# Retention and mixture of experts: the first expert round as eight block products instead of seven, with half of its second product moved ahead

## The chip, the cores and the metric

The kernel runs on one core of a Trainium2 chip. The metric is the device time of one execution in microseconds (us). An engine is named as in the profile: PE is TensorE's matmul, PEld its weight load, DVE is VectorE, ACT is ScalarE, POOL is GpSimd, SP is the engine that issues nearly all DMAs.

## The reference

```python
def _attn_ref(q, k, v):                       # q, k, v: [4, 8, 768, 64]
    gamma = 1.0 - 2.0 ** (-5.0 - np.arange(H, dtype=np.float32))
    for t in range(S):
        state = gamma[None, :, None, None] * state + np.einsum('bhd,bhe->bhde', k[:, :, t], v[:, :, t])
        y[:, :, t] = scale * np.einsum('bhd,bhde->bhe', q[:, :, t], state)

def _moe_ref(x, domain_probs, w1, w2):        # x: [3072, 512], w1: [4, 512, 1024], w2: [4, 1024, 512]
    p = domain_probs / (domain_probs.sum(-1, keepdims=True) + 1e-09)
    for e in range(E):
        h = np.maximum(x @ w1[e], 0.0)
        out += p[:, e:e + 1] * (h @ w2[e])
```

The retention's output, 4 batches of 768 tokens with 512 features, is the x of the mixture of experts.

## The kernel before, in words

**Retention.** A batch goes through in 6 chunks of 128 tokens. For a chunk, PE makes the scores (`ps_s`, L145), DVE masks them (`sp`, L148), PE makes the values (`ps_v`, L186 from the state of the chunk before, L192 from the scores) and the new state (L159), and DVE scales the values into `xr` (L201) and adds up the state (L165). POOL scales the chunk's v (`kv`, L133) and decays the state (`yst`, L171).

**Experts.** An expert's 1024 hidden features are cut into 4 slices of 256, so a batch has 16 rounds. In a round, x of the batch is a 2x2 of blocks (feature half c, token half j of 384 tokens), and the round's slice of w1 a 2x2 of blocks (hidden half f, feature half c). A round's first product takes seven block products in place of eight: sums and differences of the w1 blocks (`s`, by `combine_w1`, L271 to L274 on POOL) and of the x blocks (`t1`, `t2`, `t4` and a difference in place in `xr`, by `combine_x`, L218) go in, and the seven results are added up. Every operand is split into a high part (ACT copies it to fp32r: `xh` L242, `w1h` L283, `w2h` and `c2h` L292) and a low part (the rest, by a subtraction on DVE or POOL: `xl` L246, `w1l` L288, `w2l` and `c2l` L296). One block product is 2 times 3 matmuls (high by high, low by high, high by low) of 128x384 (`p1`, L518). Four of the seven results are completed with what came before: ACT sets three aside (`u`, L425), DVE adds (L431), ACT applies the ReLU (`hh`, L445), DVE makes its low part (`hl`, L446).

A round's second product (`p2`, L553) is 6 tiles of 128 tokens, each of 6 matmuls of 128x512 into one of two banks of `ps_o`; DVE scales a tile by the gate `pm` into `acc` (L559 in the first round, L561 after it), which frees the bank. A tile of token half j needs only the two hidden blocks of that half. In the first batch the tiles of round n are spread between the block products of round n+1 (tiles 3, 4, 5, 0, 1, 2). Weights once split are saved to DRAM by SP (L308, L312) and read back in the batches 1 to 3, in which the second product too takes seven block products.

**The order.** Every engine works through one queue, in the order in which the code is written (`manual_schedule`). The main loop calls, for each step of a round, `pass_step` (deferred pieces), `p1`, a `p2` tile, `weights` (the next round's weights: combined, split, loaded, saved) and steps of the next batch's retention. Around the change the order is this: the loop over the first batch's chunks, in which the weights of round 0 and x's blocks 1 and 2 are prepared as well; then `combine_x` for the three chunks of a half; then the high and low parts of `t1`, `t2` and the other x blocks; then round 0 in the order FIRST = 1, 2, 5, 6, 7, 3, 4, with the rest of the preparation in `weights(0, k)`; then round 1.

Of the kernel before, what the change touches and what calls it, by code (L numbers as in the profile page):

```python
# [14 lines left out]
C = 128  # L15
# [19 lines left out]


SEQ = (1, 5, 6, 2, 7, 3, 4)
FIRST = (1, 2, 5, 6, 7, 3, 4)
A_AT = {1: 0, 2: 1, 4: 2, 5: 3, 6: 4, 3: 5, 7: 6}

# [14 lines left out]
def retention_moe(ctx: ExitStack, tc: tile.TileContext, qk, kv, w1, w2, probs, probt, cmask, cqs, cks, cys, out, out_t):  # L57
# [175 lines left out]
            src = xcomb[b][{5: 0, 6: 1, 4: 2}[i]]  # L233
        return src[:, :, o]

    def x_hi(b, i, o=slice(0, HB)):
        if (b, i) not in xt:
            xt[b, i] = (
                x_p.tile([128, 2, HB], F32R, tag="xh", name="xh"),
                x_p.tile([128, 2, HB], F32R, tag="xl", name="xl"),  # L240
            )
        nc.scalar.activation(out=xt[b, i][0][:, :, o], in_=x_part(b, i, o), func=ACTF.Copy)  # L242

    def x_lo(b, i, o=slice(0, HB), eng=nc.vector):
# [40 lines left out]
    def w1_lo(n, part, eng):  # L285
        t, o = w1_part(n, part)
        hi, lo = wt1[n]
        eng.tensor_tensor(out=lo[:, o, :], in0=t, in1=hi[:, o, :].bitcast(F32), op=ALU.subtract)  # L288
# [47 lines left out]
    def weights(n, k):  # L336

        m = n + 1
        if n == 0:
            if k == 0:  # L340
                x_hi(0, 3)
                x_lo(0, 3, eng=nc.gpsimd)
                x_hi(0, 7)
                x_lo(0, 7)
                x_hi(0, 4)
                x_lo(0, 4)
                combine_w1(1, nc.gpsimd)
            elif k == 3:
                kept.pop("c11")()
            elif k == 4:  # L350
                w1_lo(1, 0, nc.vector)
            elif k == 5:
                w1_hi(1, 1)
                w1_lo(1, 1, nc.gpsimd)
                lo2(0, wt2, nc.vector)
                first_gates()
                save_w1(0)
            elif k == 6:
                combine_w2(0, nc.gpsimd)
                save_w2(0, wt2, 0)  # L360
            return
        if k == 0:
            if n == 1:
                save_w1(1)
            hi2(n - 1, wc2, "c2")
            if m < NRND:
                load_w1(m + 1)
                combine_w1(m, nc.gpsimd)
                w1_hi(m, 0)
        elif k == 1:  # L370
            lo2(n - 1, wc2, nc.vector)
            load_w2(n)
            if m < NRND:
                w1_lo(m, 0, nc.gpsimd)
        elif k == 2:
            save_w2(n - 1, wc2, 4)
            if n == 2:
                gates()
        elif k == 3 and m < NRND:
            w1_hi(m, 1)  # L380
        elif k == 4:
            hi2(n, wt2, "w2")
            if m < NRND:
                w1_lo(m, 1, nc.gpsimd)
        elif k == 5:
# [113 lines left out]
    def p1(n, i):  # L499
# [22 lines left out]
        if i == 1:  # L522
            kept[1] = act_copy(ps)
        elif i == 2:
            kept["c11"] = lambda: hidden(n, (0, 0), add(ps, kept.pop(1)))
            if n:
                kept.pop("c11")()
        elif i == 5:
            kept[5] = act_copy(ps)
        elif i == 6:  # L530
            kept[2] = act_copy(ps)
        elif i == 3:
            hidden(n, (0, 1), add(ps, kept.pop(2)))
# [128 lines left out]
    with tc.manual_schedule():  # L662
# [27 lines left out]
        for ci in range(NCHB):  # L690
            old = ci > 0
            scores(ci)
            if ci == 5:
                combine_x(0, 0, nc.vector, None, 0)
            if old:
                values(ci - 1, ci < NCHB - 1)
            else:
                state(ci)()
            if ci + 1 < NCHB:
                scale_v(ci + 1)  # L700
                decay(ci + 1)
            if ci == 1:
                w1_hi(0, 0)
                combine_w1(0, nc.gpsimd)
            elif ci == 2:
                w1_hi(0, 1)
                w1_lo(0, 0, nc.gpsimd)
            elif ci == 3:
                for i in (1, 2):
                    x_hi(0, i)  # L710
            elif ci == 4:
                x_lo(0, 1, eng=nc.gpsimd)
                w1_lo(0, 1, nc.gpsimd)
                x_lo(0, 2)
                w1_hi(1, 0)
# [1 line left out]
                load_w1(2)  # L717
                load_qk(6)
                load_kv(6)
        start[0] = False  # L720
        combine_x(0, 1, nc.vector, None, 0)
        values(ci, False)
        combine_x(0, 2, nc.vector, None, 0)
        for i in (5, 6):
            x_hi(0, i)
            x_lo(0, i)
        for c in range(3):
            combine_x(0, c, None, nc.gpsimd, 1)

        steps = iter(())  # L730
        for n in range(NRND * B):
            g, r = divmod(n, NRND)
            if r == 0 and g + 1 < B:
                steps = att_steps(g + 1)
# [1 line left out]
            if n == NRND:  # L736
# [117 lines left out]
```

## Time and profile before

| | |
|---|---|
| median of 3 runs | 1072.93 us (1072.18 to 1073.88) |
| the profiled execution | 1072.22 us |
| its span | 1070.4 us |
| PE busy | 1050.0 us, 98% |
| DVE, POOL, ACT busy | 724.8, 668.4, 375.3 us |
| mean granted TensorE clock | 0.990 of full speed |

The span runs from the first to the last instruction of the profiled execution; 1.8 us of its time lie around it. In a row of the timeline stand the start, the duration, the engine, the line, the operation, what it writes and reads, its size and how many; in square brackets, how long the engine had been idle before it and what ended that. Matmuls overlap in the pipeline, so what one costs is the distance of two starts, not its duration. In a row of the windows stand the busy time and the instructions of each engine, then the granted clock, the share in which the DMA engines were busy, and GB/s.

### The profile page before, as it was taken

The numbers are of one execution on the slowest core, as the hardware profiler recorded it, in microseconds if no ns is written. First come the engines' busy times: TensorE is split into PE (matmuls) and PEld (weight loads), VectorE is DVE, ScalarE is ACT, GpSimd is POOL, SyncE is SP. The second block draws the span as 40 slices with busy tenths as digits, with TensorE's granted clock in tenths as the row PEclk, the third lists the DMA queues.
The fourth block names the chain that finished last, engine by engine and source line by source line (L and its number), as shares of the span: only waits on it lengthen the run. The fifth ranks groups of instructions, "written<-read, shape, count | busy, mean of one in ns | idle before, by whom it ended". The sixth has DMA issues, their size and how long they took to land.

```text
span 1070.4 us, 18485 instructions
## 1 busy us (share of the span) xinstructions
PE 1050.0 (98%) x6708; PEld 996.0 (93%) x6708; DVE 724.8 (68%) x1191; ACT 375.3 (35%) x721; POOL 668.4 (62%) x638
## 2 busy tenths in 40 slices
PE   8799999999999999999999999999999999999998
PEld 6588888888889999999999999999999999999998
DVE  4866766776776576676688467676669746676664
ACT  2344443343444422223253432322224343323320
POOL 5776766767656655556479654655658865555561
PEclk9799999999999999999999999999999999999999
DMA  9499999999979777878778986877778887777783
GB/s 336 160 322 348 306 330 305 305 328 307 338 230 349 251 262 263 279 266 268 248 246 273 322 270 231 277 275 251 237 245 273 282 273 259 254 265 258 260 266 100
DMA packets 154170, 292.13 MB, mean 273 GB/s; under 512 B 12640, under 2 KB 77280, under 8 KB 154080
## 3 DMA queue, kind: packets, MB, share of 16 engines
q1 hardware_dynamic: 153360, 290.09, 80.5%
q8 instruction: 54, 0.88, 0.3%
q10 hardware_dynamic: 720, 0.86, 0.2%
q14 instruction: 36, 0.29, 0.1%
HBM read 221.64 MB, written 69.26 MB: 272 GB/s over the span
## 4 chain that ended last, share of the span: by engine, by line
PE 90%; DVE 5%; POOL 2%; DMA 1%; issue 1%; ACT 1%; ACTq 0%; POOLq 0%; DVEq 0%
PE ps_u L579 30%; PE ps_x L518 23%; PE ps_z L518 12%; PE ps_o L553 11%; PE ps_y L518 6%; PE ps_v L192 2%; PE ps_s L145 2%; PE ps_u L598 1%; PE ps_v L186 1%; DVE sum L610 1%; PE ps_v L159 1%; DVE ol L458 1%; DMA kv<-in_kv 1%; DVE sum L431 1%; DVE t L218 1%
## 5 line engine op out<-in xcount | busy, mean ns | idle before, releaser
L579 PE MATMUL ps_u<-oh,v 128*128 128x384 f32 x1288 | 379.1, 334 | 2.2 <-DVE sum L431 2.2
L469 POOL TENSOR_TENSOR b<-b 128x384 f32<-128x384 f32 x184 | 195.8, 1064 | 182.4 <-DVE b L467 151.9
L431 DVE TENSOR_TENSOR sum<-ps_u,sum 128x384 f32<-128x384 f32 x288 | 158.5, 551 | 135.1 <-PE ps_u L579 122.0
L579 PEld LDWEIGHTS ps_u<-oh,v 128*128 128x128 f32 x1288 | 237.1, 188 | 3.4 <-DVE sum L431 3.1
L458 POOL TENSOR_TENSOR ol<-b,oh 128x384 fp32r<-128x384 f32 x188 | 197.1, 1067 | 62.6 <-ACT oh L453 56.4
L453 ACT ACTIVATE oh<-b 128x384 fp32r<-128x384 f32 x330 | 160.6, 519 | 211.8 <-DVE b L467 114.4
L518 PE MATMUL ps_x<-xh,v 128*128 128x384 f32 x768 | 227.7, 337 | 0.4 <-DMA v<-k 0.2
L579 PE MATMUL ps_u<-ol,v 128*128 128x384 f32 x644 | 215.1, 334 | 0.0
L425 ACT ACTIVATE u<-ps_x 128x384 f32<-128x384 f32 x128 | 62.8, 490 | 254.1 <-PE ps_x L518 253.9
L458 DVE TENSOR_TENSOR ol<-b,oh 128x384 fp32r<-128x384 f32 x142 | 131.2, 924 | 23.1 <-ACT oh L453 23.1
L518 PEld LDWEIGHTS ps_x<-xh,v 128*128 128x128 f32 x768 | 141.4, 188 | 3.3 <-ACT u L425 0.9
L518 PE MATMUL ps_x<-xl,v 128*128 128x384 f32 x384 | 128.4, 334 | 0.0
L579 PEld LDWEIGHTS ps_u<-ol,v 128*128 128x128 f32 x644 | 120.9, 188 | 0.0
L518 PE MATMUL ps_z<-xh,v 128*128 128x384 f32 x384 | 113.9, 337 | 0.7 <-DMA v<-k 0.7
L561 DVE SCALAR_TENSOR_TENSOR acc<-ps_o,pm,acc 128x512 f32<-128x512 f32 x90 | 66.9, 744 | 36.8 <-PE ps_o L553 36.7
L553 PE MATMUL ps_o<-w2l,hh 128*128 128x512 f32 x192 | 76.4, 398 | 0.6 <-DVE w2l L296 0.6
L553 PE MATMUL ps_o<-w2h,hl 128*128 128x512 f32 x192 | 76.3, 397 | 0.0
L553 PE MATMUL ps_o<-w2h,hh 128*128 128x512 f32 x192 | 75.7, 394 | 0.3 <-DVE acc L561 0.3
L518 PEld LDWEIGHTS ps_z<-xh,v 128*128 128x128 f32 x384 | 70.7, 188 | 2.1 <-DVE b L467 1.0
L518 PEld LDWEIGHTS ps_x<-xl,v 128*128 128x128 f32 x384 | 72.1, 188 | 0.1
L518 PE MATMUL ps_z<-xl,v 128*128 128x384 f32 x192 | 64.2, 334 | 0.0
L431 DVE TENSOR_TENSOR ps_y<-ps_y,u 128x384 f32<-128x384 f32 x64 | 36.1, 564 | 33.0 <-PE ps_y L518 32.8
(108 smaller groups left out, 1685.8 us busy)
## 6 DMA issues: line engine op xcount, KB each, us to landing
v<-k SPq DMA_DIRECT2D x336, 256.0 KB, 3.1
v<-k SPq DMA_DIRECT2D x165, 512.0 KB, 4.2
k<-w1h SPq DMA_DIRECT2D x16, 896.0 KB, 6.6
k<-w1l SPq DMA_DIRECT2D x16, 896.0 KB, 6.4
qk<-in_qk SPq DMA_DIRECT2D x24, 512.0 KB, 5.6
kv<-in_kv SPq DMA_DIRECT2D x23, 512.0 KB, 6.3
w1r<-in_w SPq DMA_DIRECT2D x16, 512.0 KB, 7.0
w2r<-in_w SPq DMA_DIRECT2D x16, 512.0 KB, 4.2
```

Of the source, the lines that this page charges most:

```text
L145: nc.tensor.matmul(ps[r][:, p, :], lhsT=a[rows, 1, p, :], rhs=a[rows, 0, p, :], start=True, stop=True)
L159: nc.tensor.matmul(y[64 * r:64 * r + 64, p, :], lhsT=v[:, 0, h, :], rhs=v[:, 1, h, :], start=(bank is None), stop=True, skip_group_check=True,
L192: nc.tensor.matmul(ps[r][64 * k:64 * k + 64, half, :], lhsT=v[:, 1, h, :], rhs=sp[:, h, :], start=(c == 0 and half == 0), stop=True, skip_ ...
L425: nc.scalar.activation(out=t, in_=ps, func=ACTF.Copy)
L431: nc.vector.tensor_tensor(out=o, in0=ps, in1=u, op=ALU.add)
L453: nc.scalar.activation(out=hi, in_=t, func=ACTF.Copy)
L458: eng.tensor_tensor(out=lo, in0=t, in1=hi.bitcast(F32), op=ALU.subtract)
L469: sub = lambda o, a, b: nc.gpsimd.tensor_tensor(out=o, in0=a, in1=b, op=ALU.subtract)
L518: nc.tensor.matmul(ps, lhsT=lhsT[:, cs], rhs=rhs[:, kt, :], start=(fresh and m == 0), stop=(m == 5), skip_group_check=True,)
L553: nc.tensor.matmul(ps, lhsT=a[:, ts], rhs=b[:, fs, :], start=(m == 0), stop=(m == 5))
L561: nc.vector.scalar_tensor_tensor(out=acc[nt], in0=ps, scalar=sc, in1=acc[nt], op0=ALU.mult, op1=ALU.add)
L579: nc.tensor.matmul(ps, lhsT=w[:, r, l, ds], rhs=o, start=(m == 0), stop=(m == 5))
```

## The change

The first round is taken out of the main loop and written out ahead of it.

- `whole(f, j)` makes a hidden block of round 0 from x's and w1's blocks themselves: 2 block products, 12 matmuls, in one bank; then `hidden` takes the ReLU and the low part straight from that bank, with nothing set aside and nothing added. Four blocks make 48 matmuls where `p1` had 42. One block of w1, which no `p1` product uses alone, gets parts of its own (`first_a21`: a copy on ACT, a subtraction on POOL).
- x's second token half is split as it is, into the tiles 7 and 3, in an early piece (two chunks) and a late one (one chunk). `combine_x` and the parts of `t1`, `t2`, `t4` and of the difference in tile 7 come after it, among the four `whole` calls and behind them; the last two are only used in round 1.
- Tiles 0, 1 and 2 of round 0's second product come right behind its first product, and round 1 keeps the tiles 3, 4 and 5.
- In the loop over chunks, `decay` of the next chunk is written behind that pass's weight work. `lo2(0)` (w2's low part) moves from DVE's place late in round 0 to the place ahead of the last chunk's values. `w1_lo(1, 0)` moves from DVE to POOL, `x_lo(0, 7)` too, `x_lo(0, 3)` from POOL to DVE. Tile pairs for x are allotted in the order SEQ.

```diff
-FIRST = (1, 2, 5, 6, 7, 3, 4)
+WHOLE = ((0, 0), (1, 0), (0, 1), (1, 1))
+X_AT = {(0, 0): 1, (1, 0): 2, (0, 1): 7, (1, 1): 3}
...
+    def whole(f, j):
+        key = f, j
+        pool, tag = {(0, 0): (ps_x, "x"), (1, 0): (ps_y, "y"), (0, 1): (ps_z, "z"), (1, 1): (ps_x, "x")}[key]
+        ps = pool.tile([128, 512], F32, tag=tag, name="ps_h")[:, 0:HB]
+        m = 0
+        for c in range(2):
+            if (f, c) == (1, 0):
+                wh, wl = (a21[0][:, i, :] for i in range(2))
+            else:
+                wh, wl = (t[:, f + c, :] for t in wt1[0])
+            xh, xl = xt[0, X_AT[c, j]]
+            for kt in range(2):
+                cs = slice(kt * 128, kt * 128 + 128)
+                for lhsT, rhs in ((wh, xh), (wh, xl), (wl, xh)):
+                    nc.tensor.matmul(ps, lhsT=lhsT[:, cs], rhs=rhs[:, kt, :], start=(m == 0), stop=(m == 11))
+                    m += 1
+        hidden(0, key, ps)
...
             if ci + 1 < NCHB:
                 scale_v(ci + 1)
-                decay(ci + 1)
             if ci == 1:
                 w1_hi(0, 0)
+                first_a21(0)
                 combine_w1(0, nc.gpsimd)
...
+            if ci + 1 < NCHB:
+                decay(ci + 1)
         start[0] = False
-        combine_x(0, 1, nc.vector, None, 0)
+        early, late = slice(0, 2 * C), slice(2 * C, HB)
+        x_lo(0, 1, eng=nc.gpsimd)
+        for i in (7, 3):
+            x_hi(0, i, early)
+        lo2(0, wt2, nc.vector)
+        x_lo(0, 7, early, nc.gpsimd)
+        x_lo(0, 3, early)
         values(ci, False)
+        for i in (7, 3):
+            x_hi(0, i, late)
+            x_lo(0, i, late)
+        combine_w1(1, nc.gpsimd)
+        whole(*WHOLE[0])
+        w1_hi(1, 1)
+        w1_lo(1, 1, nc.gpsimd)
+        w1_lo(1, 0, nc.gpsimd)
+        for c in range(2):
+            combine_x(0, c, nc.vector, None, 0)
+        whole(*WHOLE[1])
         combine_x(0, 2, nc.vector, None, 0)
-        for i in (5, 6):
-            x_hi(0, i)
-            x_lo(0, i)
+        x_hi(0, 5)
+        first_gates()
+        whole(*WHOLE[2])
+        x_lo(0, 5)
+        x_hi(0, 6)
+        whole(*WHOLE[3])
         for c in range(3):
             combine_x(0, c, None, nc.gpsimd, 1)
-
-        steps = iter(())
-        for n in range(NRND * B):
+        p2(0, 0)
+        x_lo(0, 6)
+        for i in (1, 2):
+            p2(0, i)
+        for i in (7, 4):
+            x_hi(0, i)
+        x_lo(0, 7, eng=nc.gpsimd)
+        combine_w2(0, nc.gpsimd)
+        save_w1(0)
+        save_w2(0, wt2, 0)
+
+        steps = att_steps(1)
+        due = -1.0 + ATT_STEPS / 13
+        for n in range(1, NRND * B):
```

DVE, from block 2's low part in the last pass of the chunk loop (`xl<-xr`, 128x768) on, before (`t_434` is t1, `t_435` t2, `t_436` t4):

```order
L246 TENSOR_TENSOR xl<-xr,xh 128x768
L148 TENSOR_TENSOR sp<-ps_s,mask 128x4x128 x2
L218 TENSOR_TENSOR t_434<-xr 128x2x128
L218 TENSOR_TENSOR t_435<-xr,t_434 128x2x128
L201 TENSOR_TENSOR xr<-ps_v,qs 128x2x128 x2
```

and in the changed kernel, to the first hidden block's low part:

```order
L253 TENSOR_TENSOR xl<-xr,xh 128x768
L152 TENSOR_TENSOR sp<-ps_s,mask 128x4x128 x2
L205 TENSOR_TENSOR xr<-ps_v,qs 128x2x128 x2
L314 TENSOR_TENSOR w2l<-w2r,w2h 128x1024
L253 TENSOR_TENSOR xl<-xr,xh 128x2x256
L205 TENSOR_TENSOR xr<-ps_v,qs 128x2x128 x2
L253 TENSOR_TENSOR xl<-xr,xh 128x2x128 x2
L442 SCALAR_TENSOR_TENSOR hl<-ps_h,hh 128x384
```

The fifth chunk's values (the first `xr` row) no longer stand behind two differences, and w2's low part with two pieces of x's low parts has come in.

DVE again, what stands between the second hidden block's low part and the first `acc` in the changed kernel (`t_521` is t1, `t_522` t2, `t_523` t4; four differences stand ahead of it):

```order
L442 SCALAR_TENSOR_TENSOR hl<-ps_h,hh 128x384
L222 TENSOR_TENSOR t_521<-xr 128x2x128
L222 TENSOR_TENSOR t_522<-xr,t_521 128x2x128
L391 TENSOR_REDUCE ptot<-pr 128x6
L392 TENSOR_SCALAR ptot<-ptot 128x6
L393 RECIPROCAL prec<-ptot 128x6
L394 TENSOR_TENSOR pm<-pr,prec 128x24
L442 SCALAR_TENSOR_TENSOR hl<-ps_h,hh 128x384
L253 TENSOR_TENSOR xl<-t_521,xh 128x768
L442 SCALAR_TENSOR_TENSOR hl<-ps_h,hh 128x384
L571 TENSOR_SCALAR acc<-ps_o,pm 128x512
L253 TENSOR_TENSOR xl<-t_522,xh 128x768
```

where before the first `acc` had these rows ahead of it:

```order
L431 TENSOR_TENSOR ps_z<-ps_z,u 128x384
L446 SCALAR_TENSOR_TENSOR hl<-ps_z,hh 128x384
L296 TENSOR_TENSOR w2l<-w2r,w2h 128x1024
L395 TENSOR_REDUCE ptot<-pr 128x6
L396 TENSOR_SCALAR ptot<-ptot 128x6
L397 RECIPROCAL prec<-ptot 128x6
L398 TENSOR_TENSOR pm<-pr,prec 128x24
L446 SCALAR_TENSOR_TENSOR hl<-ps_x,hh 128x384
L559 TENSOR_SCALAR acc<-ps_o,pm 128x512
```

The first `acc`, which frees a bank for the third `p2` tile, now has x's differences and t1's low part ahead of it in the queue.

POOL, from the decay of the last chunk's state on, before:

```order
L171 TENSOR_TENSOR yst_115<-yst_115,ys 128x256
L246 TENSOR_TENSOR xl<-xr,xh 128x768
L288 TENSOR_TENSOR w1l<-s,w1h 128x1024
L218 TENSOR_TENSOR xr<-xr 128x2x128
L218 TENSOR_TENSOR t_436<-xr,t_435 128x2x128
```

and in the changed kernel:

```order
L295 TENSOR_TENSOR w1l<-s,w1h 128x1024
L175 TENSOR_TENSOR yst_115<-yst_115,ys 128x256
L253 TENSOR_TENSOR xl<-xr,xh 128x768
L253 TENSOR_TENSOR xl<-xr,xh 128x2x256
L278 TENSOR_TENSOR s<-w1r 128x256
L279 TENSOR_TENSOR s<-s,w1r 128x256
L280 TENSOR_TENSOR s<-w1r,s 128x256
L281 TENSOR_TENSOR s<-w1r 128x256
L295 TENSOR_TENSOR w1l<-s,w1h 128x1024
L295 TENSOR_TENSOR w1l<-w1r,w1h 128x768
L222 TENSOR_TENSOR xr<-xr 128x2x128
L222 TENSOR_TENSOR t_523<-xr,t_522 128x2x128
```

Round 0's last `w1l` has moved ahead of the decay, and round 1's weights (`s` and both `w1l`) have moved ahead of x's differences.

More of the change, by code (lines that the diff above doesn't have):

```diff
@@ L234, in x_part, with x_tiles @@
         return src[:, :, o]
-    def x_hi(b, i, o=slice(0, HB)):
+    def x_tiles(b, i):
         if (b, i) not in xt:
@@ L241, in x_hi @@
             )
+    def x_hi(b, i, o=slice(0, HB)):
+        x_tiles(b, i)
         nc.scalar.activation(out=xt[b, i][0][:, :, o], in_=x_part(b, i, o), func=ACTF.Copy)
@@ L288, in w1_lo, with first_a21 @@
         eng.tensor_tensor(out=lo[:, o, :], in0=t, in1=hi[:, o, :].bitcast(F32), op=ALU.subtract)
+    a21 = []
+    def first_a21(part):
+        t = raw1[0][:, 0, :]
+        if part == 0:
+            a21.append(v1_p.tile([128, 2, 256], F32R, tag="v1", name="a21"))
+            nc.scalar.activation(out=a21[0][:, 0, :], in_=t, func=ACTF.Copy)
+        else:
+            nc.gpsimd.tensor_tensor(out=a21[0][:, 1, :], in0=t, in1=a21[0][:, 0, :].bitcast(F32), op=ALU.subtract)
     def hi2(n, d, tag):
@@ L338, in weights @@
         m = n + 1
[L339 to L361, printed above, removed]
         if k == 0:
@@ L364, in weights @@
                 save_w1(1)
+                x_lo(0, 4)
             hi2(n - 1, wc2, "c2")
@@ L524, in p1 @@
         elif i == 2:
-            kept["c11"] = lambda: hidden(n, (0, 0), add(ps, kept.pop(1)))
-            if n:
-                kept.pop("c11")()
+            hidden(n, (0, 0), add(ps, kept.pop(1)))
         elif i == 5:
@@ L538, in p1 @@
             hidden(n, (1, 0), ps)
+    def whole(f, j):
[6 more added lines that the diff above has]
+                wh, wl = (a21[0][:, i, :] for i in range(2))
+            else:
+                wh, wl = (t[:, f + c, :] for t in wt1[0])
[6 more added lines that the diff above has]
+        hidden(0, key, ps)
     acc = {}
@@ L692, in retention_moe @@
             scores(ci)
-            if ci == 5:
-                combine_x(0, 0, nc.vector, None, 0)
             if old:
@@ L708, in retention_moe @@
             elif ci == 3:
+                for i in SEQ:
+                    x_tiles(0, i)
                 for i in (1, 2):
                     x_hi(0, i)
+                first_a21(1)
             elif ci == 4:
-                x_lo(0, 1, eng=nc.gpsimd)
                 w1_lo(0, 1, nc.gpsimd)
@@ L740, in retention_moe @@
                 fetch_gate(n)
-            tiles = [3, 4, 5, 0, 1, 2] if 0 < n <= NRND else []
+            tiles = [3, 4, 5, 0, 1, 2] if n <= NRND else []
+            if n == 1:
+                tiles = [3, 4, 5]
             q, first = divmod(n, 2)
-            for k, i in enumerate(SEQ if n else FIRST):
+            for k, i in enumerate(SEQ):
                 t = 7 * n + k
```

## The prediction

> **What bounds the kernel now.** I read the page first: busy shares, then the chain that ended last.
>
> ```profile
> PE 1050.0 (98%) x6708; PEld 996.0 (93%) x6708; DVE 724.8 (68%) x1191; ACT 375.3 (35%) x721; POOL 668.4 (62%) x638
> PE 90%; DVE 5%; POOL 2%; DMA 1%; issue 1%; ACT 1%; ACTq 0%; POOLq 0%; DVEq 0%
> ```
>
> PE is the bound, except where the 5% of DVE and the 2% of POOL in the chain lie. The windows of 20 us show where: the first two rows are the end of the first batch's retention and the first round; from 60 us on PE is busy at full clock (last columns: granted clock, DMA share, GB/s).
>
> ```profile
> 20.00:40.00 20.00, 16.03 (x198) 13.34 (x193) 17.41 (x25) 8.52 (x12) 18.49 (x16) 0.80 0.80 258
> 40.00:60.00 20.00, 16.38 (x63) 14.20 (x62) 14.42 (x19) 6.58 (x12) 15.28 (x15) 0.77 0.49 156
> 60.00:80.00 20.00, 20.00 (x111) 17.70 (x110) 14.98 (x24) 8.11 (x13) 13.13 (x13) 1.00 0.95 322
> ```
>
> Then PE's timeline through that stage: the last chunk's values, the first block product, the gaps, and neighbours that tell what a matmul costs.
>
> ```profile
> 27.26 0.67 PE L186 MATMUL ps_v<-qk,yst 64*64 64x128 f32 x16
> 28.89 0.45 PE L518 MATMUL ps_x<-xh,w1h 128*128 128x384 f32 x1
> 32.47 0.66 PE L518 MATMUL ps_y<-xh,w1h 128*128 128x384 f32 x1 [2.24 <-DVE xr L201]
> 32.92 0.52 PE L518 MATMUL ps_y<-xl,w1h 128*128 128x384 f32 x1
> 33.24 0.52 PE L518 MATMUL ps_y<-xh,w1l 128*128 128x384 f32 x1
> 45.62 0.41 PE L518 MATMUL ps_x<-xh,w1h 128*128 128x384 f32 x1
> 51.62 0.44 PE L518 MATMUL ps_z<-xh,w1l 128*128 128x384 f32 x1 [2.36 <-POOL w1l L288]
> 53.54 0.63 PE L553 MATMUL ps_o<-w2h,hh 128*128 128x512 f32 x1
> 53.97 0.63 PE L553 MATMUL ps_o<-w2l,hh 128*128 128x512 f32 x1
> 55.78 0.45 PE L518 MATMUL ps_x<-xh,w1h 128*128 128x384 f32 x1
> 56.41 0.39 PE L553 MATMUL ps_o<-w2h,hh 128*128 128x512 f32 x1
> 58.84 0.40 PE L553 MATMUL ps_o<-w2h,hh 128*128 128x512 f32 x1
> 60.23 0.33 PE L518 MATMUL ps_x<-xh,w1h 128*128 128x384 f32 x1
> 61.28 0.40 PE L553 MATMUL ps_o<-w2h,hh 128*128 128x512 f32 x1
> ```
>
> By the distances of starts, six 128x384 matmuls cost 61.28 - 60.23 = 1.05, one 0.173 us, and a `p2` tile of six 128x512 costs 60.23 - 58.84 = 1.39. After the gap of 2.24 us one costs 0.32 (33.24 - 32.92), until 45.6; after that of 2.36 a 128x512 soon costs 0.43, until 55.8. Between 28.89 and 56.41 PE does 42 matmuls of round 0, 18 of round 1 and one tile: 60 x 0.173 + 1.39 = 11.8 us of work in 27.5. So 15.7 us are lost to gaps and the low clock, and the change can win only from these. It adds six matmuls, 1.0 us.
>
> **What DVE and POOL cost each other.** The changed order is dense on both, so this decides the sum.
>
> ```profile
> 36.13 2.37 DVE L246 TENSOR_TENSOR xl<-t,xh 128x768 fp32r<-128x768 f32 x2 [0.45 <-ACT xh L242]
> 36.23 1.45 POOL L218 TENSOR_TENSOR t<-xr,t 128x256 f32<-128x256 f32 x1
> 42.33 0.55 DVE L431 TENSOR_TENSOR ps_y<-ps_y,u 128x384 f32<-128x384 f32 x1
> 48.67 2.90 POOL L288 TENSOR_TENSOR w1l<-s,w1h 128x1024 fp32r<-128x1024 f32 x1 [4.18 <-ACT w1h L283]
> 49.50 2.10 DVE L396 TENSOR_SCALAR ptot<-ptot 128x6 f32<-128x6 f32 x1
> ```
>
> A DVE instruction on 6 elements takes 2.10 us and ends at 51.60, just behind POOL's `w1l` (51.57): operations of DVE between SBUF tiles and POOL's run one at a time. At 36 us they take turns: POOL's 0.7 us piece waits for DVE's first and runs between the two. An operation with an operand in PSUM (42.33) isn't held up. What the others cost, mostly alone:
>
> ```profile
> 20.48 0.61 POOL L171 TENSOR_TENSOR yst<-yst,ys 128x256 f32<-128x256 f32 x1
> 24.41 1.04 POOL L133 TENSOR_TENSOR kv<-kv,ks 128x512 f32<-128x512 f32 x1
> 27.05 1.81 POOL L246 TENSOR_TENSOR xl<-xr,xh 128x768 fp32r<-128x768 f32 x1
> 52.34 0.74 POOL L302 TENSOR_TENSOR w2r<-w2r 128x256 f32<-128x256 f32 x1
> 61.16 2.41 POOL L288 TENSOR_TENSOR w1l<-s,w1h 128x1024 fp32r<-128x1024 f32 x1 [0.79 <-ACT w1h L283]
> 21.98 0.41 DVE L165 TENSOR_TENSOR yst<-ps_v,yst 128x256 f32<-128x256 f32 x1
> 25.67 0.95 DVE L246 TENSOR_TENSOR xl<-xr,xh 128x768 fp32r<-128x768 f32 x1
> 26.54 1.28 DVE L148 TENSOR_TENSOR sp<-ps_s,mask 128x512 f32<-128x512 f32 x2
> 33.24 0.43 DVE L218 TENSOR_TENSOR t<-xr,t 128x256 f32<-128x256 f32 x1
> 33.59 0.74 DVE L201 TENSOR_TENSOR xr<-ps_v,qs 128x256 f32<-128x256 f32 x2
> 48.16 1.22 DVE L296 TENSOR_TENSOR w2l<-w2r,w2h 128x1024 fp32r<-128x1024 f32 x1
> 60.64 0.74 DVE L559 TENSOR_SCALAR acc<-ps_o,pm 128x512 f32<-128x512 f32 x1
> 13.22 0.84 ACT L283 ACTIVATE w1h<-w1r 128x768 fp32r<-128x768 f32 x1 [8.60 <-DMA w1r<-in_w]
> 47.55 1.05 ACT L283 ACTIVATE w1h<-s 128x1024 fp32r<-128x1024 f32 x1
> ```
>
> Starts of neighbours lie up to 0.08 us closer than these durations, or as much farther apart for POOL's pieces that depend on each other. No row has the early pieces' 128x512 split; between the 256 and the 768 rows (POOL 0.74 to 1.81, DVE 0.43 to 0.95) I take 1.2 and 0.6.
>
> **Step 1, the chunk loop: 0.8 us worse.** With the decays behind the weight work, POOL starts to combine w1 when it lands, at 13.2 (ACT's row): 3.1 for four pieces, then decay 0.6, `kv` 1.0, `w1l` 1.8, decay 0.6, `kv` 1.0 and the new block's low part 0.7 give 22.0; the next decay waits for DVE's state (21.98 + 0.41), then `kv`: 24.1. So the 128x1024 `w1l` runs from 24.1 to 26.5, where DVE wants the port at 25.7 for block 2's low part. That ends at 27.4 instead of 26.6. The last decay, behind both, ends at 28.0, and PE starts the last chunk's values then instead of at 27.26; the masked scores (27.4 + 1.2) come late too. The first product starts at 29.7 instead of 28.9. If the two operations miss each other, the step costs nothing.
>
> **Step 2, the first product: the gap of 2.24 us and the low clock after it go.** That gap was `ps_y` waiting for the fifth chunk's values, on DVE behind t1 and t2, which waited for POOL; now they stand right behind the scores (29.3). The first two hidden blocks need only x's blocks 1 and 2: 24 x 0.173 = 4.2 us, to 33.9. The third needs x's second half complete. DVE: w2's low part behind POOL's `xl` (28.0 to 29.8), to 30.9; POOL's early piece, to 32.1; DVE's early piece, to 32.7; the last chunk's values, to 33.4; ACT's late pieces, by 33.9; DVE's late pieces in turn with POOL's combining, to 34.6 for tile 7 and 35.6 for tile 3. PE waits 0.5 us for the first and not for the second. The 48 matmuls end at 38.7.
>
> On the clock: 2.24 us of idleness were enough to lose it. [...]
>
> **Step 3, the third p2 tile: a new wait of 5.7 us.** The first tile wants the second block's `hl`, which stands on DVE behind four differences. POOL's two `w1l` of round 1 (2.41, then 1.81) can start at 37.5, when ACT has the high part, and from there DVE gets one turn between two of POOL's: the fourth difference from 40.0 to 40.4, `hl` to 40.9. PE waits 1.1 us for that and has two tiles done at 42.6. The third wants a bank of `ps_o` back, that is the first `acc`. Ahead of it on DVE: the fifth difference behind the second `w1l`, to 42.6; the sixth one POOL piece later, to 43.7; the gate's four small operations, two of which wait for a POOL piece, to 45.3; `hl`, to 45.9; t1's low part behind one more piece, to 46.9; `hl`, to 47.5; `acc`, to 48.3. So PE idles from 42.6 to 48.3 and comes back at the low clock. That held from about 52.6 to 55.8 after the gap of 2.36; at 3.3 us it costs 1.7. From 48.3 on come the tile (2.6), 12 matmuls of round 1, its first tile and 6 more, which end at 55.7. Behind the waiting tile stands all of PE's queue.
>
> **The sum.** Before, PE had one tile done at 56.41; now it has four at 55.7: 0.7 + 3 x 1.39 = 4.9 us less. The other way round: of the 15.7 us lost, 0.8 + 0.5 + 1.1 + 5.7 + 1.7 and the 1.0 of the six matmuls remain, 10.8. Moving tiles costs nothing in itself.
>
> Does the rest of the kernel keep it? What POOL, ACT and SP bring to the next rounds comes at about the old time, and PE asks 4.9 us earlier. The tightest is round 2's second `w1l`, which landed at 61.16 + 2.41 = 63.6 for this use:
>
> ```profile
> 69.88 0.33 PE L518 MATMUL ps_z<-xh,w1h 128*128 128x384 f32 x1
> SPq L312 <- DVE ptot L395: 16.8, 1, 16.8
> ```
>
> 6.3 us of slack, of which 4.9 go. SP's queue, with the saves of rounds 0 and 1 and the next loads, stood 16.8 us at w2's low part; that is now made at 31 instead of 49.4, so the DMAs have more time, not less. The profiled execution becomes 1072.2 - 4.9 = 1067.3, and by the median 1072.93 - 4.9 = **1068.0 us**. Below, 0.2% is 2.1 us, about what a measurement of this kernel can tell from no change.
>
> **Rivals.** *The port is kinder.* If the fourth and fifth difference fall into POOL's pause before 37.5, `acc` comes 2.4 to 4 us sooner. Then POOL's own queue limits: from 28.0 it holds low parts of x (1.8, 1.2, 1.8), twelve combining pieces (9.2), six differences (4.3) and four `w1l` (8.4), 26.7 us up to round 2's second `w1l`, and about 9 of DVE's turns between: 63.8. Asked for at 69.9 before, that allows 6.1 us: 1066.8. If the two hardly held each other up, the 5.7 and 1.7 would go whole, 7.4 more than forecast: 1060.6. For it: turns are a matter of 0.1 us. Against: the row of 2.10 us.
>
> *Slower: POOL keeps the port.* If POOL's queued operations follow each other and DVE gets in only where POOL waits, then w2's low part waits from 29.3 to 34.1, PE has 3.3 us of gap at the third block, and t1's low part comes behind tile 7's new low part (1.8) and w2's combining (3.1) too: I work `acc` out at 57.2. Each us after 53.2 is a loss, so 57.2 gives 1072.9 + 4.0 = 1077. Against it stand the turns at 36 us. [...]
>
> *No change.* PE gains its 4.9 us and gives them back in the rounds 1 and 2, because POOL's queue without a pause runs some 5 us later than I have it and PE then waits for `w1l`: 1072 to 1073.
>
> **The numbers.** The forecast 0.52, with 1066 to 1070 as its own range (`acc` 2 us either way); the kinder port 0.20; no change 0.14; POOL keeps the port 0.14, of which 0.01 lies within 0.2%. So faster 0.72, same 0.15, slower 0.13. The range starts at 1064, between the two prices of the kinder port, and ends at 1073.5, which leaves out most of the slower case.
>
> **What would show it.** Right: 48 matmuls 0.173 us apart from about 29.7 on, with no gap over 1 us; the third tile waiting some 5 us for `acc`, near 48; a granted clock of 0.5 only behind that; no gap on PE later. Wrong: over 2 us of gap at the third block, `acc` before 45 or after 53, or PE waiting for `w1l` in round 2.

## The result, and the profile after

| | before | after |
|---|---|---|
| median | 1073.22 us (1072.18 to 1073.88, 4 runs) | 1065.85 us (1064.77 to 1067.14, 4 runs) |
| the profiled execution, its span | 1072.22, 1070.4 us | 1065.44, 1063.6 us |
| mean granted clock | 0.990 | 0.997 |

The ratio after to before is 0.9946, with a 95% interval of 0.9934 to 0.9957. The medians lie 7.4 us apart, the two spans 6.8 us; forecast were 4.9.

The windows of the changed kernel, after those of 20 us shown of before:

```profile
20.00:40.00 20.00, 18.22 (x196) 16.22 (x194) 18.93 (x26) 8.13 (x13) 18.65 (x15) 1.00 0.93 327
40.00:60.00 20.00, 15.65 (x78) 13.65 (x76) 13.83 (x22) 8.63 (x14) 19.19 (x18) 0.83 0.47 143
60.00:80.00 20.00, 19.25 (x113) 16.90 (x110) 15.49 (x24) 8.16 (x14) 12.25 (x13) 1.00 1.06 362
```

PE's granted clock is 1.00 from 20 to 40 us (0.80 before). What changed most from 40 to 60 us is POOL: 19.19 us busy, against 15.28. It now works with next to no pause.

PE's timeline of the changed kernel:

```profile
27.02 0.78 PE L190 MATMUL ps_v<-qk,yst 64*64 64x128 f32 x16 [1.78 <-POOL yst L175]
28.76 0.45 PE L548 MATMUL ps_h<-xh,w1h 128*128 128x384 f32 x1
33.05 0.34 PE L548 MATMUL ps_h<-xh,w1h 128*128 128x384 f32 x1
33.38 0.41 PE L548 MATMUL ps_h<-xl,w1h 128*128 128x384 f32 x1
37.45 0.40 PE L565 MATMUL ps_o<-w2h,hh 128*128 128x512 f32 x1
44.73 0.80 PE L565 MATMUL ps_o<-w2h,hh 128*128 128x512 f32 x1 [4.35 <-DVE acc L571]
50.67 0.39 PE L565 MATMUL ps_o<-w2h,hh 128*128 128x512 f32 x1
53.10 0.40 PE L565 MATMUL ps_o<-w2h,hh 128*128 128x512 f32 x1
```

The first product starts at 28.76, its 48 matmuls end at 37.45 with one pause of about 0.16 us (33.05 to 33.38), two `p2` tiles follow, and the third waits 4.35 us for `acc`. It and the 12 matmuls behind it take 50.67 - 44.73 = 5.94 us, most of it at the half clock (0.51 from 45 to 50 us), where 1.39 + 12 x 0.173 = 3.47 are their price: 2.5 us lost. At 53.10 PE stands where it stood at 56.41, with three tiles more done: 3.31 + 3 x 1.39 = 7.5 us. DVE and POOL behind these rows:

```profile
23.58 2.92 DVE L253 TENSOR_TENSOR xl<-xr,xh 128x768 fp32r<-128x768 f32 x1
32.35 1.75 DVE L253 TENSOR_TENSOR xl<-xr,xh 128x256 fp32r<-128x256 f32 x2 [0.16 <-ACT xh L249]
34.50 0.49 DVE L222 TENSOR_TENSOR t<-xr 128x256 f32<-128x256 f32 x1
35.82 0.42 DVE L222 TENSOR_TENSOR t<-xr,t 128x256 f32<-128x256 f32 x1
36.21 0.56 DVE L442 SCALAR_TENSOR_TENSOR hl<-ps_h,hh 128x384 fp32r<-128x384 f32 x1
36.69 2.10 DVE L222 TENSOR_TENSOR t<-xr 128x256 f32<-128x256 f32 x1
38.83 1.95 DVE L222 TENSOR_TENSOR t<-xr,t 128x256 f32<-128x256 f32 x1
43.94 0.73 DVE L571 TENSOR_SCALAR acc<-ps_o,pm 128x512 f32<-128x512 f32 x1
```

```profile
23.33 2.35 POOL L295 TENSOR_TENSOR w1l<-s,w1h 128x1024 fp32r<-128x1024 f32 x1
33.79 0.92 POOL L281 TENSOR_TENSOR s<-w1r 128x256 f32<-128x256 f32 x1
35.88 2.62 POOL L295 TENSOR_TENSOR w1l<-s,w1h 128x1024 fp32r<-128x1024 f32 x1 [1.18 <-ACT w1h L290]
38.48 2.02 POOL L295 TENSOR_TENSOR w1l<-w1r,w1h 128x768 fp32r<-128x768 f32 x1
51.00 0.73 POOL L322 TENSOR_TENSOR w2r<-w2r 128x256 f32<-128x256 f32 x1
57.86 2.39 POOL L295 TENSOR_TENSOR w1l<-s,w1h 128x1024 fp32r<-128x1024 f32 x1 [0.42 <-ACT w1h L290]
```

In the chunk loop DVE's block 2 (23.58, 0.95 us before) stood behind POOL's `w1l`. Four differences of x (34.50 to 36.24) ran in POOL's pause of 1.18 us; the fifth and the sixth, 0.42 us alone, took 2.10 and 1.95 beside POOL's `w1l`. POOL's own pause ahead of round 1's `w1l` had been 4.18 us before (at 48.67, in the prediction's rows): ACT then made the high part behind a ReLU of round 0; now it makes it as soon as POOL has combined w1.

Of the 7.5 us, 0.75 go in round 2, where PE now waits for an `acc`. The changed kernel's row, and then the same tile of before, which had no wait:

```profile
74.08 0.51 PE L565 MATMUL ps_o<-w2h,hh 128*128 128x512 f32 x1 [0.75 <-DVE acc L573]
```

```profile
80.66 0.40 PE L553 MATMUL ps_o<-w2h,hh 128*128 128x512 f32 x1
```

80.66 - 74.08 = 6.6 us are left there, near the difference of the spans, 6.8. What changes later evens out: at the start of the second batch a wait of 0.58 us for w2's low part goes (before, at 310.52), and PE's waits for DMAs behind it grow by about as much.

### The profile page after: what moved, and what is told of

Read it like the earlier page. It is cut to its first block, busy times and chain, and to the rows that moved or that the text cites. A ratio compares the mean times of both kernels' runs of the same rounds, so it can differ in the third digit from the quotient of the medians.

```text
span 1063.6 us, 18494 instructions
## 1 busy us (share of the span) xinstructions
PE 1044.9 (98%) x6714; PEld 992.5 (93%) x6714; DVE 721.9 (68%) x1189; ACT 376.6 (35%) x722; POOL 672.7 (63%) x641
## 4 chain that ended last, share of the span: by engine, by line
PE 89%; DVE 7%; DMA 1%; ACT 1%; issue 1%; POOL 1%; ACTq 0%; DVEq 0%; POOLq 0%
PE ps_u L591 30%; PE ps_x L514 23%; PE ps_z L514 12%; PE ps_o L565 10%; PE ps_y L514 6%; PE ps_s L149 2%; PE ps_v L196 2%; PE ps_u L610 1%; PE ps_v L190 1%; DVE sum L622 1%; DVE ol L454 1%; PE ps_v L163 1%; DVE xl L253 1%; DMA kv<-in_kv 1%; DVE sum L427 1%
```

## The experiments

Twelve kernels, each beside the kernel before on the same chip, in three groups of four. The first four below are one group, the next four another, and the third holds the last two and the two with 3 extra products. The median of before was 1072.28, 1072.09 and 1072.50 us in them. A kernel of the second or third group is set against the changed kernel's 1065.17 of the first; where the ratios to before give another difference, it stands beside.

**The changed kernel again**, unchanged.

> The changed kernel itself, unaltered. Theory A (the gain is the round-0 stage: gaps and low clock gone, a wait for acc instead): again 6 to 8 us below the kernel before, 1065 to 1067. Theory B (part of the recorded gain is chance: the kernel before was profiled with the chunk loop at half clock from 10 to 15 us, the changed one without, 2.1 us earlier at the last state): over five rounds the gain shrinks to 5 us or less, and the granted clock differs from run to run.

Measured: 1065.17 us (1064.38 to 1066.45), ratio 0.9937 (0.9925 to 0.9950). The gain stands, by the medians 7.1 us; the smaller gain of theory B doesn't come, though the granted clock does differ from run to run, from 0.995 to 0.998. This profile took 1066.45 us. From 10 to 16 us it and the first one differ, here the first one and then this:

```profile
10.00:16.00 6.00, 6.00 (x128) 5.45 (x122) 4.08 (x8) 1.15 (x2) 5.05 (x7) 1.00 1.04 415
```

```profile
10.00:16.00 6.00, 6.00 (x66) 5.54 (x68) 1.84 (x4) 1.15 (x2) 5.12 (x7) 0.50 1.03 412
```

The same program kept the full clock behind PE's first gap in one execution and lost it in the other; they lie 1.0 us apart. The other runs on record fit that: of the changed kernel's nine, the four with a mean granted clock of 0.997 or 0.998 took 1064.4 to 1065.4 us, the five with 0.995 took 1065.2 to 1067.1.

**A third bank for the third tile**, so that it needn't wait for `acc`.

```diff
-        ps = ps_o.tile([128, DM], F32, tag="o", name="ps_o")
+        if n == 0 and i == 2:
+            ps = ps_a.tile([128, DM], F32, tag="a", name="ps_o")
+        else:
+            ps = ps_o.tile([128, DM], F32, tag="o", name="ps_o")
```

> The third tile goes to a bank of ps_a, which is idle then, so it needs no acc. Theory A (the wait of 4.35 us and the 4.9 us at half clock behind it, 2.4 more, are on the path): the gap at 40 us goes; but ACT's copies stand behind c2h (51.8) and round 2's second w1l lands at 60.3 for a use at 62.4, so only 1 to 3 us of the 6.8 are kept: 1063 to 1065. Rival (POOL's queue sets the end of round 0 and 1 anyway): within 0.5 us of the changed kernel.

Measured: 1065.52 us (1064.87 to 1066.22), ratio 0.9938 (0.9925 to 0.9952). The wait for `acc` and the half clock behind it are gone, 4.35 and 2.5 us (the granted clock is 1.00 from 40 to 60 us), and the time is the same. I had expected 1063 to 1065. What came instead, PE first, then ACT and POOL of this kernel:

```profile
48.36 0.45 PE L514 MATMUL ps_x<-xh,w1h 128*128 128x384 f32 x1 [1.10 <-ACT u L421]
55.31 0.44 PE L514 MATMUL ps_x<-xh,w1h 128*128 128x384 f32 x1 [1.81 <-ACT u L421]
```

```profile
47.83 0.47 ACT L421 ACTIVATE u<-ps_x 128x384 f32<-128x384 f32 x1
52.71 1.06 ACT L310 ACTIVATE c2h<-w2r 128x1024 fp32r<-128x1024 f32 x1 [4.40 <-POOL w2r L322]
54.41 0.47 ACT L421 ACTIVATE u<-ps_z 128x384 f32<-128x384 f32 x1
54.78 0.48 ACT L421 ACTIVATE u<-ps_x 128x384 f32<-128x384 f32 x1
```

```profile
51.94 0.73 POOL L322 TENSOR_TENSOR w2r<-w2r 128x256 f32<-128x256 f32 x1
```

PE waits twice for a copy `u`. The second of them (54.78) stands on ACT behind `c2h`, and that waits for the last of POOL's sums of w2 (52.67); the first (47.83) stands on ACT behind two high parts of x's differences, which POOL makes. In the changed kernel the sums of w2 end at 51.73, just in time for a PE that had waited for `acc`. Two smaller waits follow, 0.51 us for `hl` at 61.56 and 1.58 us for an `acc` at 74.23. So behind the removed wait stood other chains that end at nearly the same moment.

**The three tiles back in round 1**: `p2(0, 0)` to `p2(0, 2)` taken out behind the first round, and round 1's list six tiles long again.

> Plain products kept, the three tiles back in round 1. Theory A (the plain products win the time; the tiles only fill a wait): 1 to 4 us slower than the changed kernel, 1067 to 1070, with a gap at 37.5 for round 1's w1l instead of one at 40.2 for acc. Rival (the moved tiles are what pays, 3 x 1.39 put into PE's idle time): 1071 or more, nearly the kernel before.

Measured: 1067.72 us (1067.19 to 1068.43), ratio 0.9960 (0.9947 to 0.9972), 2.55 us over the changed kernel beside it. PE's gap moves as theory A had it, from `acc` to round 1's low part:

```profile
41.42 0.58 PE L514 MATMUL ps_x<-xh,w1l 128*128 128x384 f32 x1 [2.53 <-POOL w1l L295]
```

That is what moving the tiles is worth beside the plain products; the other 4.6 us of the 7.1 come with the rest of the change, the plain products and the new order, which no run takes apart.

**w1's low part moved out of the chunk loop**, so that PE needn't wait for the last decay.

```diff
             elif ci == 4:
-                w1_lo(0, 1, nc.gpsimd)
                 x_lo(0, 2)
...
         x_lo(0, 7, early, nc.gpsimd)
+        w1_lo(0, 1, nc.gpsimd)
         x_lo(0, 3, early)
```

> The last low part of round 0's w1 moves on POOL from the chunk loop to behind x's early piece, so the last decay doesn't wait for it. Theory A (step 1 is on the path: PE waits 1.8 us for the decay): 1 to 2 us faster than the changed kernel, 1064 to 1065, and block 2's low part on DVE takes 0.95 instead of 2.92. Rival (POOL's queue as a whole is the bound, and only its order changes): within 0.5 us of the changed kernel.

Measured: 1067.09 us (1065.68 to 1067.88), ratio 0.9953 (0.9941 to 0.9966): slower than the changed kernel by 1.9 us, which neither theory had. DVE's block 2 took 0.95 us, where the changed kernel has 2.92, and PE didn't wait for the decay. But POOL now stood waiting for DVE's state; its rows, and PE's behind them:

```profile
25.67 1.19 POOL L175 TENSOR_TENSOR yst<-yst,ys 128x256 f32<-128x256 f32 x1 [1.56 <-DVE yst L169]
30.84 2.84 POOL L295 TENSOR_TENSOR w1l<-s,w1h 128x1024 fp32r<-128x1024 f32 x1
```

```profile
46.95 0.79 PE L565 MATMUL ps_o<-w2h,hh 128*128 128x512 f32 x1 [5.75 <-DVE acc L571]
```

POOL pauses where it had worked on w1, and pays with the same work later, in turns with DVE: its `w1l` takes 2.84 us here and 2.35 in the changed kernel. PE's third tile then waits 5.75 us for `acc` instead of 4.35. So I formed the theory that the following runs test: POOL's queue, with its turns with DVE, sets the end of the first two rounds.

**Two low parts back on DVE**, to relieve POOL.

```diff
-        w1_lo(1, 0, nc.gpsimd)
...
         combine_x(0, 2, nc.vector, None, 0)
+        w1_lo(1, 0, nc.vector)
...
-        x_lo(0, 7, eng=nc.gpsimd)
+        x_lo(0, 7)
```

> The changed kernel with two low parts that it had given to POOL back on DVE: round 1's w1 low part of 128x768 (behind the fifth difference of x) and the new low part of x's tile 7 (behind round 0's last tile). Each took 1.8 to 2.0 us on POOL in the changed kernel and 0.95 us on DVE where nothing disturbed it. Theory A (POOL's queue and the turns at the port set the end of the first two rounds): POOL has 3.8 us less, the last differences and w2's sums come 2 to 3.5 us earlier, and the time falls by 0.5 to 2 us against the changed kernel's 1065.2, to 1063.2 to 1064.7. Theory B (DVE's queue sets it, since the first two tiles' gate scalings stand on DVE behind all of this): the first gate scaling (acc), at 43.9 in the changed kernel, comes 1 us later, the wait of 4.35 us becomes 5.3, and the time is 1066 to 1067.

Measured: 1066.71 us (1065.04 to 1067.68), ratio 0.9954 (0.9942 to 0.9967): no gain, as theory B had it. The rows of DVE and then of POOL:

```profile
46.06 0.73 DVE L571 TENSOR_SCALAR acc<-ps_o,pm 128x512 f32<-128x512 f32 x1
```

```profile
49.23 0.73 POOL L322 TENSOR_TENSOR w2r<-w2r 128x256 f32<-128x256 f32 x1
59.75 2.38 POOL L295 TENSOR_TENSOR w1l<-s,w1h 128x1024 fp32r<-128x1024 f32 x1 [3.77 <-ACT w1h L290]
```

The first row of each in the repeated profile of the changed kernel, which has the same half clock at the start (0.50 from 12 to 16 us in both):

```profile
45.85 0.73 DVE L571 TENSOR_SCALAR acc<-ps_o,pm 128x512 f32<-128x512 f32 x1
```

```profile
52.92 0.73 POOL L322 TENSOR_TENSOR w2r<-w2r 128x256 f32<-128x256 f32 x1
```

So POOL's chain is 3.7 us shorter and DVE's 0.2 longer, and the time follows DVE's. What POOL won it spends in a pause of 3.77 us in round 2, and PE waits for none of that: this pause costs nothing.

**Both chains shortened**: the third bank and the two low parts together, and in round 1 the high part `c2h` one step later, behind the `u` copy of ps_z, with the low part and the next load of w2 one step later too. Of the edit, what is new here:

```diff
-            hi2(n - 1, wc2, "c2")
+            if n > 1:
+                hi2(n - 1, wc2, "c2")
...
-            lo2(n - 1, wc2, nc.vector)
-            load_w2(n)
+            if n > 1:
+                lo2(n - 1, wc2, nc.vector)
+                load_w2(n)
             if m < NRND:
                 w1_lo(m, 0, nc.gpsimd)
+            if n == 1:
+                hi2(0, wc2, "c2")
         elif k == 2:
+            if n == 1:
+                lo2(0, wc2, nc.vector)
+                load_w2(1)
```

> The same two low parts on DVE, the third tile of round 0's second product in a bank that the first batch's values no longer use (so it needn't wait for acc), and the high and low part of w2's sums one and one step later in round 1, so that ACT's copies of round 1's results don't stand behind POOL's sums. Theory A (POOL's queue sets the end of the first two rounds; with the third bank alone the won time was waited for at round 1's u copies, 0.56, 1.10 and 1.81 us, behind an ACT operation that waited 4.40 us for POOL): those waits go, and the time is 2 to 4 us under the changed kernel's 1065.2, 1061 to 1063.2. Theory B (the time is set by what comes after, as round 2's w1 low part or the loads of the second batch): the waits move to round 2 and the time stays within 1 us, 1064.2 to 1066.

Measured: 1062.75 us (1061.88 to 1063.51), ratio 0.9920 (0.9907 to 0.9932), 2.4 us under the changed kernel's 1065.17 (1.8 by the ratios), where the third bank alone and the two low parts alone had given nothing. All four runs lie below all nine of the changed kernel. PE keeps the full clock from 40 to 60 us; below it stands ACT's first `u` of round 1:

```profile
40.00:60.00 20.00, 18.03 (x98) 15.04 (x97) 17.21 (x26) 10.19 (x17) 18.36 (x16) 1.00 0.58 179
```

```profile
45.44 0.47 ACT L428 ACTIVATE u<-ps_x 128x384 f32<-128x384 f32 x1
```

The time is the one of theory A. POOL's shorter chain has a part in it: with the third bank alone this `u` came at 47.83, and the last chunk's values started at 27.79 there and at 27.20 here, so it comes 1.8 us sooner by the values. PE's wait of 1.10 us for it is gone, and the later `c2h` can't have done that, as it stands on ACT behind this copy in both kernels. The wait of 1.81 us is gone too; how much of that is the later `c2h` stays open, since it wasn't run by itself.

**The decay back in its old place**, ahead of each pass's weight work (`decay(ci + 1)` behind `scale_v` again).

> The changed kernel with the decay of the state back in its old place, ahead of each pass's weight work on POOL. Theory A (POOL's queue is the bound, and PE's 1.78 us wait for the last decay costs nothing by itself, as the run with w1's low part moved showed): POOL pauses for DVE's state ahead of its weight work instead of filling that time, so its w1 and x work ends 0.5 to 1.5 us later, PE's wait for the decay goes, and the time is 1065.2 to 1067. Theory B (PE's wait for the decay and the late first product count, as my first step had it): the first product starts 0.8 to 1.8 us earlier and the time falls by as much, to 1063.4 to 1064.4.

Measured: 1066.45 us (1065.30 to 1069.72), ratio 0.9959 (0.9945 to 0.9973): by the medians of the two groups 1.3 us over the changed kernel (2.4 by the ratios), within the range of theory A and against theory B. The intervals of the two ratios overlap, so that it costs anything is likely and not shown. The profile is of the slowest of the six runs, 1069.72 us, with the half clock (0.50) from 10 to 16 us, so its waits may be longer than those of a run near the median. POOL's row for the decay that the changed kernel puts behind the combining of w1, and PE's at the third block:

```profile
17.39 0.61 POOL L175 TENSOR_TENSOR yst<-yst,ys 128x256 f32<-128x256 f32 x1 [3.82 <-DVE yst L169]
```

```profile
34.03 0.69 PE L548 MATMUL ps_h<-xl,w1h 128*128 128x384 f32 x1 [2.90 <-POOL xl L253]
```

POOL stands 3.82 us for DVE's state (2.89 us before, where the clock from 10 to 16 us was 0.72), time in which the changed kernel combines w1. PE's wait for the last decay is gone, and one of 2.90 us for POOL's `xl` comes instead.

**The first gap filled with 12 products** (results not used).

```diff
+            if ci == 0:
+                for w in (384,) * 12:
+                    nc.tensor.matmul(wps[:, 0:w], lhsT=warm[:, 0:128], rhs=warm[:, 0:w], start=True, stop=True)
```

> The changed kernel with 12 extra products of 128x384 on TensorE behind the first chunk's scores (their results are not used), which fill the idle time before the first state, so that the clock isn't lost there. The changed kernel's one profile kept the clock at 10 to 16 us (1065.44), the other lost it (1066.45), so this gap decides by chance. Theory A (the low clock there costs about the 1.0 us between these two profiles, where it falls): the low clock at 10 to 16 us is never seen and the median is 0.3 to 1.0 us lower, 1064.2 to 1064.9. Theory B (the first round is bound by POOL's queue, which the clock hardly touches): within 0.3 us of 1065.2.

Measured: 1070.16 us (1068.25 to 1073.76), ratio 0.9988 (0.9975 to 1.0000). Neither theory: I had made the filler far too long.

```profile
8.18 8.01 PE L707 MATMUL ps_w<-warm 128*128 128x384 f32 x24
16.11 0.69 PE L163 MATMUL ps_y<-kv 128*64 128x64 f32 x16
```

In the plain fp32 form the 12 products are 24 records and take 8.01 us; the first state comes at 16.11 instead of 10 us. The miss tells one thing: 6 us of delay at the start cost 5.0 us at the end, so the chunk loop has little slack, about 1 us of 6.

**The first gap filled with 3 products**, otherwise the same edit.

> The changed kernel with 3 extra products of 128x384 in the fp32 form behind the first chunk's scores (results not used): by the run with 12 of them, which took 8.01 us, some 2.0 us, that fit the idle 2.3 to 2.7 us before the first state. Theory A (the low clock at 10 to 16 us, which fell in one profile of the changed kernel and not in the other, costs about 1 us where it falls): never seen there, median 1064.2 to 1064.9, and the runs lie closer together than 1 us. Theory B (it costs nothing, or the extra products delay the first state): 1065.1 or more.

Measured: 1064.25 us (1063.95 to 1065.14), ratio 0.9931 (0.9918 to 0.9944), 0.9 us under the changed kernel by the medians (0.6 by the ratios, whose intervals overlap). Its profile has a granted clock of 1.00 from 10 to 16 us, all six runs have a mean granted clock of 0.997 or 0.998, and they lie 1.2 us apart, against 2.1; under 1 us was expected. That is theory A, and its price of about 1 us fits the changed kernel's nine runs above.

**The same 3 products in the kernel with both chains shortened.**

> The kernel with the two low parts on DVE, the third bank and the later c2 parts, and the same 3 extra products as the run beside it. Theory A (the gains add up): 1061.3 to 1062.3, the fastest of all. Theory B (with POOL relieved the early clock no longer matters, since the first rounds wait elsewhere): 1062.5 to 1063.

Measured: 1062.33 us (1061.62 to 1062.47), ratio 0.9910 (0.9897 to 0.9924): the fastest of all. Against 1062.75 that doesn't decide between the two theories, but the runs lie 0.85 us apart instead of 1.63.

**The kernel before, with one ACT operation one place up**: round 1's w1 high part ahead of the third block's ReLU. POOL's low part is written with it, and passes no other work of POOL.

```diff
             elif k == 4:
+                w1_hi(1, 1)
+                w1_lo(1, 1, nc.gpsimd)
                 w1_lo(1, 0, nc.vector)
             elif k == 5:
-                w1_hi(1, 1)
-                w1_lo(1, 1, nc.gpsimd)
```

> The kernel before, with one ACT operation of its first round moved one place up: the high part of round 1's combined w1 (128x1024) ahead of the ReLU of the third hidden block. In the kernel before POOL stood idle 4.18 us for that operation (its w1l at 48.67), and PE then 0.68 and 2.36 us for POOL, the second with the half clock after it. Theory A (a pause of POOL in the first two rounds is paid in full): w1l starts 2 to 2.4 us earlier, PE's two waits shrink to under 1 us together, and the time falls by 2 to 4 us against the 1072.1 of the kernel before, to 1068 to 1070. Theory B (the first round was bound by PE at the half clock and DVE's chain, and POOL's pause cost nothing): within 1 us of 1072.1.

Measured: 1068.77 us (1067.25 to 1070.69), ratio 0.9969 (0.9959 to 0.9980), 3.7 us under before by the medians and 3.3 by the ratio. POOL's pause and PE's wait, the rows of this kernel:

```profile
46.40 2.67 POOL L288 TENSOR_TENSOR w1l<-s,w1h 128x1024 fp32r<-128x1024 f32 x1 [1.72 <-ACT w1h L283]
```

```profile
48.48 0.45 PE L518 MATMUL ps_z<-xh,w1h 128*128 128x384 f32 x1 [0.43 <-DVE hl L446]
```

The pause falls from 4.18 to 1.72 us, and PE's waits of 0.68 and 2.36 become one of 0.43. The time is that of theory A: the pause shrank by 2.5 us, PE's waits for what follows it by 2.6, and the half clock behind the longer of them went too (0.86 granted from 40 to 60 us, 0.77 before). Here POOL's pause and PE's waits are one event, so the run shows that it lay on the path and not which of the two to count.

**The kernel before, with its gap of 2.24 us filled** by 12 products of 0.173 us behind the first block product.

```diff
                 p1(n, i)
+                if n == 0 and k == 0:
+                    spare = ps_z.tile([128, 512], F32, tag="z", name="ps_w")
+                    for _ in range(12):
+                        nc.tensor.matmul(spare[:, 0:HB], lhsT=wt1[0][0][:, 0, 0:128], rhs=xt[0, 1][0][:, 0, :], start=True, stop=True)
```

> The kernel before, with 12 extra products of 128x384 (0.173 us each, results not used) on PE in its gap of 2.24 us behind the first block product, so that the clock isn't lost there. Theory A (of what the plain products won, a part is the half clock from 32.5 to 45.6 us): the granted clock stays at 1.00 through 32 to 46 us, the four hidden blocks come 1 to 3 us earlier and with them the w1 high part that ACT makes behind them, and the time is 1069 to 1071. Theory B (DVE and POOL set the pace of that round whatever the clock): PE waits more often instead, and the time is within 0.8 us of 1072.1.

Measured: 1071.73 us (1069.71 to 1073.44), ratio 0.9999 (0.9990 to 1.0008). Nothing, as theory B had it, though the clock stayed up some 6 us longer. The windows of this kernel, and PE's row at 36.46:

```profile
32.00:36.00 4.00, 1.87 (x10) 1.25 (x8) 3.93 (x8) 0.43 (x1) 3.27 (x5) 1.00 0.91 305
36.00:40.00 4.00, 2.98 (x11) 2.32 (x12) 3.35 (x3) 4.00 (x7) 3.66 (x3) 0.82 0.28 95
40.00:44.00 4.00, 3.42 (x11) 2.91 (x11) 3.44 (x4) 1.08 (x3) 3.84 (x4) 0.50 0.00 0
```

```profile
36.46 0.44 PE L518 MATMUL ps_z<-xh,w1h 128*128 128x384 f32 x1 [2.38 <-ACT xh L242]
```

At full clock PE was merely ready sooner for the next operand: it waits 2.38 us, where it had waited 1.43, and then loses the clock anyway. A mean of 0.82 from 36 to 40 us puts that at 38.6 (1.4 of 4 us at the half clock). So the half clock from 32.5 to 38.6 cost nothing here; what it cost from there to 45.6 stays open, since the clock fell there again.

## Why the prediction was right, and where it was not

**Direction.** Faster, as forecast; but the gain is half as large again, 7.1 to 7.4 us by the medians against 4.9. The time lies just under the forecast's own range of 1066 to 1070 and 1.0 us under the kinder port's 1066.8. Of that rival the first half came, differences of x in POOL's pause and an early `acc`. Its second half, by which POOL's queue then sets the time, didn't come where it was put: PE never waited for round 2's second `w1l`.

**Step 1, 0.8 us worse: the collision was there, its price wasn't.** `w1l` met DVE's block 2 as forecast and PE waited 1.78 us, yet the first product came at 28.76 and not at 29.7: in this profile the chunk loop ran at full clock (1.00 from 10 to 16 us). In the repeated profile, at the half clock there (0.50), it came at 30.69 with a wait of only 0.67 us, so what the collision itself costs stays open. Both runs that removed this wait were slower, by 1.9 and 1.3 us, the second not clear of the noise. So the wait wasn't a loss that could be won back this way: in the changed kernel POOL works during it on what PE needs next.

**Step 2: right.** The gap of 2.24 us went, the 48 matmuls run 0.173 us apart, and the third block waits 0.16 us where 0.5 was forecast. They end at 37.45, 1.25 us sooner than forecast, 0.9 of it from the earlier start.

**Step 3, the third tile's wait: the step that failed.** The prediction put `acc` at 48.3, because the fourth difference was to run from 40.0, between POOL's two `w1l`, and held a wait of 1.1 us for the second block's `hl`. All four differences were done at 36.24, most of it in POOL's pause, `hl` followed at once, and `acc` started at 43.94. The differences could start at 34.5 as DVE had finished tile 3's late piece at 34.1, not at 35.6. The wait is 4.35 us instead of 5.7, and the half clock behind it costs 2.5 instead of 1.7. Mechanism and place were right, and the two collisions that remained (2.10 and 1.95 us) are of the kind described. By the prediction's own signs this step is wrong, as `acc` came before 45; and there was a gap on PE later, the 0.75 us at 74.08. By the sum's own marker, 55.7 became 53.1: 2.6 us, of which that gap takes 0.75 again.

**What the sum took for the cost.** It counted PE's gaps and low clock and the six matmuls, 10.8 us of them left, with this wait as the largest. As a count of what differs between two profiles that holds: 7.5 us of them are gone at 53.10. As a price of one wait it doesn't: the run with the third bank took that wait and the half clock away and won nothing, and the run that kept the clock up in the gap of before won nothing. The kinder port's sentence on POOL's queue was nearer to what the third bank met, but as a time it was off: it put round 2's second `w1l` at 63.8, and that ended at 60.25, 3.5 us sooner.

**Where the gain came from.** Moving the tiles: 2.55 us, measured. The rest, some 4.6, comes with the plain products. In the kernel before, one ACT operation moved past a ReLU gave 3.3 to 3.7 us by itself, with POOL's pause of 4.18 us cut to 1.72. In the changed kernel this operation stands right behind POOL's sums, and the pause is 1.18. That the same 3 us or so are at work in both is read from these rows and not shown; the two weren't taken apart within the changed kernel.

**The other rivals.** POOL keeping the port would have shown 3.3 us of gap at the third block and `acc` at 57: 0.16 and 43.94. In the changed kernel's rows DVE got its turn between two of POOL's operations each time: its fifth difference, 0.42 us alone, took 2.10 us and ended at 38.79, 0.29 us behind the first `w1l`, and its sixth took 1.95 and ended 0.28 us behind the second. The port is the prediction's name for what the two engines take turns at; the rows show the turns, and no run shows what it is that they share. The rival *no change* would have shown PE waiting for `w1l` in round 2; none came.

## What to carry to other kernels

Where a second engine feeds the bound one nearly without a pause, cost a change by that engine's queue too: the bound engine's gaps may be cover for it, and its waits are then no list of prices. Look at the feeder's own pauses and at what ends them; here one operation in another engine's order was worth half of a large rewrite. But a pause of the feeder is no price by itself either: POOL's 3.77 us in round 2 cost nothing, as PE didn't wait for what came behind. And where a removed wait wins nothing, look for a second chain of the same length before giving it up: the third bank alone gave 0, and together with two low parts moved off POOL and one ACT copy made later it gave 2.4 us.

## What the runs showed of the hardware

What a short gap does to PE's clock differs from one execution to the next: after idle times of 2.40 and 2.37 us in front of the first state, the same program ran at 1.00 and at 0.50 from 10 to 16 us; the kernel with both chains shortened kept 1.00 after 2.66 us. PE's row there, in the changed kernel's repeat and then in the latter:

```profile
9.94 1.12 PE L163 MATMUL ps_y<-kv 128*64 128x64 f32 x16 [2.37 <-POOL kv L137]
```

```profile
9.92 0.69 PE L163 MATMUL ps_y<-kv 128*64 128x64 f32 x16 [2.66 <-POOL kv L137]
```

So a gap of 2.37 us lost the clock here, as one of 2.24 us did in the prediction's rows, and one of 2.66 us kept it. What decides between the two, no run shows.

A product of 128x384 in the plain fp32 form takes 8.01 / 12 = 0.67 us (the run with 12 extra products, granted clock 1.00 from 8 to 16 us), and in the fp32r form 0.173.
